# Routing the results of the first mixture layer by twos, and a ninth addend in the gate sums

## The chip, the core and the metric

The kernel runs on one core of one Trainium2 chip. The metric is the time of one execution on the device, in microseconds (us), as the median of several runs. The engines are named as in the profile: PE (TensorE, matrix products), PEld (its weight loads), DVE (VectorE), ACT (ScalarE), POOL (GpSimd) and SP (SyncE, which issues most of the transfers).

## The reference

```
x = attention(q, k, v)                      # a decaying state, 2 x 768 tokens, 512 wide: 1536 rows
# first layer: 8 experts, each token to one of them, if x @ w_skip > 0
probs = exp(logits - max) ; probs /= probs.sum() + 1e-9
x[mask_e] += gate * (relu(x[mask_e] @ w1[e]) @ w2[e])
# second layer: a new choice of expert from the first layer's result, at most `capacity` rows each
out[i] = gate2 * (relu(x_i @ w1b[e]) @ w2b[e])
```

So the second layer's choice (the logits of the 512 wide row, their maximum, the gate, and the place of the row in its expert's list) must be worked out for every row that leaves the first layer. This is the routing that the change is about. A router pass has 128 rows: one expert of the first layer.

## The kernel before

Attention fills the first 70 us. Then the first layer goes through its 8 experts, 128 gathered rows each, and the second layer through its 8 experts in blocks of 128 rows. All matrix products of the layers are in three passes over operands that are split into a rounded part and a rest (hi and lo, 512 columns a matmul); six of them use up one half of a weight chunk. A few weight chunks stay whole and are used in plain fp32 (L825). Weights come in chunks of 1 MB on SP's queue; ACT rounds each half (L248), DVE takes the rest (L251), and the raw buffer is then free for the next chunk. `pump` puts one such half into the order at each turn, and `step_side` calls it.

The code is written in the order in which each engine executes: every engine keeps the order of its own instructions. The loop over expert e of the first layer runs: `layer1(e)`, 24 matmuls into s; `layer2(e - 1)`, matmuls into o, with the transposes of the next expert's rows x after the first six (`turned`, L761); then the transposes of layer 1's result h (hT, eight, L761). `turned` and all routing products use one ring of three PSUM buffers, t.

`route_b(e)` routes the result of expert e. It is a generator in the list `side`: one step of it per turn, each between two groups of six matmuls. Its steps: DVE forms the result row (L846); PE transposes it (L860, four), ACT copies it (L862); PE forms the logits on 32 columns (L866), ACT copies them (L868); PE sums the four partial logits (L871), and `pick` finds maximum, choice m and gate on DVE and ACT; PE counts the place in the list (`ranked`, L327 and L328, which need m and the running count cumb); DVE turns the place into a one-hot matrix whereb (L889); PE adds row numbers to the table of slots (`to_slots`, L341). For expert e this runs beside `layer1(e + 2)`, since the result of expert e comes at the end of loop e + 1. The last two experts have a shorter course, since the second layer waits for them.

`gate` sums the eight exponentials (L320), adds 1e-9 (L322) and takes the reciprocal (L323).

Of the kernel before, what the change touches and what calls it, by code (L numbers as in the profile page):

```python
# [7 lines left out]
F32 = mybir.dt.float32  # L8
# [10 lines left out]
NTILE = NT // 128  # L19
# [22 lines left out]
def kernel(  # L42
# [88 lines left out]
    cum = const.tile([128, 2, 16], BF16, name="cum")  # L131
    cumb = const.tile([128, 8], BF16, name="cumb")
    cap = const.tile([1, 1], F32, name="cap")
    t9 = {n: const.tile([128, n, 9], F32, name=f"t9{n}") for n in (1, 2, 4)}


# [12 lines left out]
    def derived():  # L149

        for t in t9.values():
            nc.gpsimd.memset(t, 0.5)
        nc.gpsimd.memset(cum, 0.0)
# [138 lines left out]
    def pick(lg, nt, ng, rm, gate_out, ex=None, gate_first=False):  # L292

        n = nt * ng
        l4 = lg[:, :, 0:8 * ng].rearrange("p a (g j) -> p a g j", g=ng)
        mx = sm.tile([128, nt, ng, 1], F32, tag=f"mx{n}", name="mx")
        nc.vector.tensor_reduce(out=mx, in_=l4, axis=AX.X, op=ALU.max)
        d = sm.tile([128, n, 8], F32, tag=f"d{n}", name="d")
        d4 = d.rearrange("p (a g) j -> p a g j", a=nt)
        nc.vector.tensor_tensor(out=d4, in0=l4, in1=mx.to_broadcast([128, nt, ng, 8]), op=ALU.subtract)  # L300
        if rm is None:
            rm = taken(lg, nt)
        if ex is None:
            ex = sm.tile([128, n, 8], F32, tag=f"ex{n}", name="ex")
        nc.scalar.activation(out=ex, in_=d, func=ACTF.Exp)
        t = t9[n]
        nc.vector.scalar_tensor_tensor(out=t[:, :, 0:8], in0=d, scalar=0.0, in1=rm, op0=ALU.is_equal, op1=ALU.mult)
        if gate_first:
            gate(ex, nt, ng, gate_out)
        tm = sm.tile([128, n, 1], F32, tag=f"tm{n}", name="tm")  # L310
        nc.vector.tensor_reduce(out=tm, in_=t, axis=AX.X, op=ALU.max)
        m = sm.tile([128, n, 8], BF16, tag=f"m{n}", name="m", bufs=3)
        nc.vector.tensor_tensor(out=m, in0=t[:, :, 0:8], in1=tm.to_broadcast([128, n, 8]), op=ALU.is_equal)

        return m, lambda: gate(ex, nt, ng, gate_out)

    def gate(ex, nt, ng, gate_out):
        n = nt * ng
        se = sm.tile([128, nt, ng, 1], F32, tag=f"se{n}", name="se")
# [63 lines left out]
    def route_tokens(rows, rows_p):  # L383
# [94 lines left out]
        def last_chunk(xt, psum):  # L478
# [5 lines left out]
            ex = sm.tile([128, 2 * B, 8], F32, tag="exl", name="exl", bufs=1)  # L484
# [249 lines left out]
    w2_p = fast.enter_context(tc.tile_pool(name="w2", bufs=NW2))  # L734
    w_free += [(0, w2_p)] * NW2
    m_p = fast.enter_context(tc.tile_pool(name="m", bufs=2))
    row2 = [m_p.tile([128, RW], F32, name=f"row2{i}", bufs=1) for i in range(3)]
    for t in row2:
        nc.gpsimd.memset(t[:, DM:RW], 0.0)

    def psum(tag="t", bufs=3):
        return ps.tile([128, 512], F32, tag=tag, bufs=bufs, name=tag)
# [13 lines left out]
    def turned(src, g, tag, divided=True):  # L756

        pool = x_p if tag == "x" else m_p
        t = psum()
        for k in range(4):  # L760
            nc.tensor.transpose(t[:, 128 * k:128 * k + 128], src[:, 512 * g + 128 * k:512 * g + 128 * k + 128], ident)  # L761
        t = t.rearrange("p (k t) -> p k t", k=4)
        if divided:
            w = 128 if tag == "x" else 256
            hi = pool.tile([128, 4, w], F32R, tag=tag + "h", name=tag + "h")[:, :, 0:128]
            lo = pool.tile([128, 4, w], F32R, tag=tag + "l", name=tag + "l")[:, :, 0:128]
            split(t, hi, lo)
            return hi, lo
        as_is = pool.tile([128, 4, 128], F32, tag=tag + "w", name=tag + "w")
        nc.scalar.activation(out=as_is, in_=t, func=ACTF.Copy)  # L770
        return (as_is,)

# [66 lines left out]
            return True  # L839
        return uses.get(kind, 0) > 0  # L840

    def route_b(e, xs, acc, lead, rest):

        r2 = row2[e % 3]
        idc = xs[:, IDCOL:IDCOL + 1]
# [3 lines left out]
        nc.gpsimd.tensor_copy(out=r2[:, IDCOL:IDCOL + 1], in_=idc)  # L849
        if xs is not a0:  # L850
            xs_free.append(xs)
        there = sm.tile([128, 1], F32, tag="there", name="there")
        nc.gpsimd.tensor_scalar(out=there, in0=idc, scalar1=0.0, scalar2=None, op0=ALU.is_lt)
        rm = sm.tile([128, 1, 8], F32, tag="rmb", name="rmb")
        nc.gpsimd.tensor_scalar(out=rm[:, 0, :], in0=rev, scalar1=there, scalar2=None, op0=ALU.mult)
        yield
        yield from idle(lead)
        xr = psum()
        for k in range(KT):
            nc.tensor.transpose(xr[:, 128 * k:128 * k + 128], r2[:, 128 * k:128 * k + 128], ident)  # L860
        x2t = m_p.tile([128, KT, 128], F32, tag="x2t", name="x2t", bufs=1)
        nc.scalar.activation(out=x2t, in_=xr.rearrange("p (k t) -> p k t", k=KT), func=ACTF.Copy)  # L862
        yield
        lg = psum()
        for k in range(KT):
            nc.tensor.matmul(out=lg[32 * k:32 * k + 32, 0:128], lhsT=wgt[:, k, :], rhs=x2t[:, k, :], start=True, stop=True)  # L866
        lgs = sm.tile([128, 128], F32, tag="lgsb", name="lgsb")
        nc.scalar.activation(out=lgs, in_=lg[:, 0:128], func=ACTF.Copy)  # L868
        yield
        lt = psum()  # L870
        nc.tensor.matmul(out=lt[:, 0:8], lhsT=lgs, rhs=zsum[:, 8:16], start=True, stop=True)  # L871
        m, weigh = pick(lt[:, 0:8].unsqueeze(1), 1, 1, rm, r2[:, GCOL + 1:GCOL + 2].unsqueeze(1), None, e == E - 1)
        if e < E - 1:
            weigh()
        if e >= E - 2:
            write_rows(nc.scalar, r2.unsqueeze(1), 1)
        m = m[:, 0, :]
        rhs = sm.tile([128, 2, 8], BF16, tag="rhsb", name="rhsb")
        nc.gpsimd.tensor_scalar(out=rhs[:, 0, :], in0=m, scalar1=p1, scalar2=None, op0=ALU.mult)  # L879
        nc.gpsimd.tensor_scalar(out=rhs[:, 1, :], in0=m, scalar1=float(128 * (NTILE + e)), scalar2=None, op0=ALU.mult)  # L880
        yield from idle(1 + rest)
        rk = psum()
        ranked(rk, lc[:, 1, :], m, cumb)
        pr = sm.tile([128, 8], F32, tag="prb", name="prb")
        nc.vector.tensor_tensor(out=pr, in0=rk[:, 0:8], in1=m, op=ALU.mult)
        sl = sm.tile([128, 1], F32, tag="slb", name="slb")
        nc.vector.tensor_reduce(out=sl, in_=pr, axis=AX.X, op=ALU.add)
        where = sm.tile([128, 257], BF16, tag="whereb", name="whereb")
        nc.vector.tensor_scalar(out=where, in0=iota, scalar1=sl, scalar2=None, op0=ALU.is_equal)  # L889
        if e < E - 2:  # L890
            write_rows(nc.scalar, r2.unsqueeze(1), 1)
        nc.gpsimd.tensor_tensor(out=cumb, in0=cumb, in1=m, op=ALU.subtract)
        yield from idle(3 if e < E - 1 else 1)
        to_slots(where, rhs, 8, 8)
        yield

    def emit_out(xs, acc, shared=False):
# [30 lines left out]
        nc.vector.tensor_copy(out=flag, in_=over)  # L928
        return flag

    side = []
    pieces = [1]

    def step_side():
        for g in list(side):
# [27 lines left out]
        except StopIteration as stop:  # L963
            return stop.value

    def then_route(e, acc, lead, rest, between=lambda: None):
        g = route_b(e, xs1[e], acc, lead, rest)
        next(g)
        between()
        side.append(g)  # L970

    h0 = []
    first = layer1(x, "w1a", 0, h0)
# [10 lines left out]
    step_side()  # L984
    x = turned(xs1[1], 0, "x")
    acc = run(second)
    then_route(0, acc, 1, 1)
    for e in range(1, E):
        first = layer1(x, "w1a", e)
        if e == 1:  # L990
# [10 lines left out]
        if e > 1:  # L1001
            second = layer2(hT.pop(e - 1), "w2a", e - 1)
            next(second)
            step_side()
            x = turned(xs1[e + 1] if e + 1 < E else a0, 0, "x")
            if e == E - 1:

# [5 lines left out]
            then_route(e - 1, acc, *((2, 1) if e < E - 1 else (0, 0)), step_side)  # L1013
        hT[e] = run(turn)
    second = layer2(hT.pop(E - 1), "w2a", E - 1)
    for i in range(FT // 2):
# [1 line left out]
        pieces[0] = i < 2  # L1018
        step_side()
    acc = run(second)  # L1020
    last = route_b(E - 1, xs1[E - 1], acc, 0, 0)
    next(last)

    xs2 = {(0, 0): a0}

# [298 lines left out]
```

## Time and profile before

| | us |
|---|---|
| median of three runs (397.52 to 399.19) | 398.36 |
| the profiled execution | 395.72 |
| its span, first to last instruction | 393.9 |
| PE busy in it | 376.5 (96%) |
| DVE, ACT, POOL busy | 244.8, 210.5, 119.9 |

A row of the timeline has the start and the length of an instruction, engine, line and operation, result and operand, and the number of instructions merged. The ends of PE's matmuls are modelled, so what a group of PE instructions costs is read from start to start: from its first to the first of the next group.

### The profile page before, as it was taken

To read this page: it belongs to the slowest core of one execution; us is meant where nothing else is said; L and a number is where in the kernel's file an instruction comes from. 1 tells how busy PE (TensorE), PEld (TensorE's weight loads), DVE (VectorE), ACT (ScalarE), POOL (GpSimd) and SP (SyncE) were. 2 spreads that over 40 slices of the span, in tenths; PEclk is the share of its full clock that TensorE was granted. 3 is DMA by queue.
4 is the path that set the end of the run, shared out by engine and by line. 5 is a ranking of instruction groups with operands and counts; after the bars stand their busy time and mean duration, and the time that the engine had idled before them with its cause. 6 is when DMAs were issued, how large, how long until landed. Compare 5 with 4: busy or idle time off the path is not lost. (4 is left out here: it accounts for less than half of the span.)

```text
span 393.9 us, 6866 instructions
## 1 busy us (share of the span) xinstructions
PE 376.5 (96%) x2664; PEld 309.0 (78%) x2664; DVE 244.8 (62%) x437; ACT 210.5 (53%) x319; POOL 119.9 (30%) x184
## 2 busy tenths in 40 slices
PE   8999999899989999998999999999999999999992
PEld 4788887786667677676567998989989898898981
DVE  3657767498889869869535964654826476373200
ACT  1435655388778748747326753636636465462201
POOL 3678854262504402202143201304022040311102
PEclk9999999999999999999999999999999999999997
DMA  8999973899999998889844773965739377110101
GB/s 303 416 419 404 333 251 146 278 329 376 347 426 351 303 352 307 286 314 311 292 162 117 264 276 113 277 245 175 252 136 342 126 229 275 61 54 5 48 3 41
DMA packets 18175, 95.98 MB, mean 244 GB/s; under 512 B 2449, under 2 KB 2705, under 8 KB 8664
## 3 DMA queue, kind: packets, MB, share of 16 engines
q1 hardware_dynamic: 12196, 80.85, 56.5%
q0 software_dynamic: 3280, 9.76, 8.0%
q10 hardware_dynamic: 2660, 4.86, 3.3%
q8 instruction: 23, 0.38, 0.4%
q14 instruction: 16, 0.13, 0.1%
HBM read 87.03 MB, written 9.48 MB: 245 GB/s over the span
## 5 line engine op out<-in xcount | busy, mean ns | idle before, releaser
L251 DVE TENSOR_TENSOR lo<-big,hi 128x1024 fp32r<-128x1024 f32 (+1 forms) x126 | 147.5, 1185 | 60.9 <-ACT hi L248 60.0
L248 ACT ACTIVATE hi<-big 128x1024 fp32r<-128x1024 f32 (+1 forms) x126 | 124.6, 1013 | 3.8 <-DMA big<-in_w2a_dram 1.7
L784 PE MATMUL s<-xh,lo 128*128 128x256 f32 x224 | 63.4, 283 | 0.0
L783 PE MATMUL s<-xl,hi 128*128 128x256 f32 x224 | 63.4, 283 | 0.0
L782 PE MATMUL s<-xh,hi 128*128 128x256 f32 x224 | 63.4, 283 | 0.0
L905 POOL DMA_INDIRECT out_dram<-y,ixo x16 | 18.6, 1162 | 142.4 <-ACT y L900 139.4
L782 PE MATMUL o<-hi,hTh 128*128 128x512 f32 x112 | 44.9, 401 | 0.0
L783 PE MATMUL o<-lo,hTh 128*128 128x512 f32 x112 | 44.4, 396 | 0.0
L784 PE MATMUL o<-hi,hTl 128*128 128x512 f32 x112 | 44.4, 396 | 0.0
L782 PEld LDWEIGHTS s<-xh,hi 128*128 128x128 f32 x224 | 42.9, 191 | 0.3
L783 PEld LDWEIGHTS s<-xl,hi 128*128 128x128 f32 x224 | 42.9, 191 | 0.3
L784 PEld LDWEIGHTS s<-xh,lo 128*128 128x128 f32 x224 | 42.9, 192 | 0.0
L1084 ACT ACTIVATE hTh<-s 128x512 fp32r<-128x512 f32 x28 | 16.8, 598 | 41.0 <-PE s L784 41.0
L1085 DVE SCALAR_TENSOR_TENSOR hTl<-s,hTh 128x512 fp32r<-128x512 f32 x28 | 19.3, 691 | 30.5 <-ACT hTh L1084 30.3
L790 PE MATMUL s<-hi,xh 128*128 128x512 f32 x80 | 34.3, 429 | 1.6 <-DVE xl L377 0.9
L900 ACT ACTIVATE y<-o,rowc 128x512 f32<-128x512 f32 (+1 forms) x15 | 10.1, 674 | 47.6 <-issue 30.6
L790 PE MATMUL s<-lo,xh 128*128 128x512 f32 x80 | 31.5, 394 | 0.0
L879 POOL TENSOR_SCALAR rhsb<-m,cs 128x8 bf16<-128x8 bf16 x8 | 2.5, 306 | 81.1 <-DVE se L320 76.6
L790 PE MATMUL o<-hi,hTh 128*128 128x512 f32 x64 | 26.6, 415 | 0.0
L790 PE MATMUL o<-lo,hTh 128*128 128x512 f32 x64 | 25.3, 396 | 0.0
L784 PEld LDWEIGHTS o<-hi,hTl 128*128 128x128 f32 x112 | 21.1, 188 | 5.1
L790 PE MATMUL s<-hi,xl 128*128 128x512 f32 x80 | 25.1, 394 | 0.0
(162 smaller groups left out, 635.6 us busy)
## 6 DMA issues: line engine op xcount, KB each, us to landing
big<-in_w1a_dram SPq DMA_DIRECT2D x16, 1024.0 KB, 7.7
big<-in_w2a_dram SPq DMA_DIRECT2D x16, 1024.0 KB, 7.2
big<-in_w1b_dram SPq DMA_DIRECT2D x16, 1024.0 KB, 7.1
big<-in_w2b_dram SPq DMA_DIRECT2D x16, 1024.0 KB, 5.1
qk<-in_qkv_dram SPq DMA_DIRECT2D x5, 1024.0 KB, 10.2
big<-in_qkv_dram SPq DMA_DIRECT2D x5, 1024.0 KB, 12.0
table<-rowc ACTq DMA_DIRECT2D x5, 516.0 KB, 6.3
table<-row ACTq DMA_DIRECT2D x8, 258.0 KB, 7.2
```

Of the source, the lines that this page charges most:

```text
L248: nc.scalar.activation(out=hi[:, k], in_=r3[:, k], func=ACTF.Copy)
L251: nc.vector.tensor_tensor(out=lo[:, k], in0=r3[:, k], in1=hi[:, k].bitcast(F32), op=ALU.subtract)
L782: nc.tensor.matmul(out=acc, lhsT=a[0], rhs=w[0], start=first, stop=False)
L783: nc.tensor.matmul(out=acc, lhsT=a[0], rhs=w[1], start=False, stop=False)
L784: nc.tensor.matmul(out=acc, lhsT=a[1], rhs=w[0], start=False, stop=last)
L790: nc.tensor.matmul(out=acc, lhsT=a, rhs=w, start=first and i == 0, stop=last and i == len(todo) - 1)
L879: nc.gpsimd.tensor_scalar(out=rhs[:, 0, :], in0=m, scalar1=p1, scalar2=None, op0=ALU.mult)
L900: nc.scalar.activation(out=y[:, 0:n], in_=acc[:, 0:n], func=ACTF.Copy, scale=xs[:, GCOL + 1:GCOL + 2])
L905: new = nc.gpsimd.indirect_dma_start(out=out[:, :], out_offset=bass.IndirectOffsetOnAxis(ap=ix, axis=0), in_=y, in_offset=None, bounds_che ...
L1084: nc.scalar.activation(out=hi[:, g:g + 2, :], in_=acc, func=ACTF.Relu)
L1085: nc.vector.scalar_tensor_tensor(out=lo[:, g:g + 2, :], in0=acc, scalar=0.0, in1=hi[:, g:g + 2, :].bitcast(F32), op0=ALU.max, op1=ALU.subtract
```

## The change

Experts 0 and 1, and 2 and 3, are routed together, in a second list of generators, `sited`. It is stepped at two sites of each loop: just before x is transposed, and just before h is transposed. So a couple's course spreads over three loops. Experts 4 and 5 are routed together too, but in the old list and places; 6 and 7 go alone as before. The result row itself moves into a function of its own and stays where it was. The rows of two experts stand side by side in a tile (two tiles for two, in place of three for one), and each step works on both: eight transposes, two copies, logits 256 columns wide, two sums, one choice. The count for the second expert of a couple is the running count less the first one's choice, so `ranked` now needs a GpSimd subtraction that itself needs m (tile cu). In the gate sums the exponentials stand in a tile with a ninth column that holds 1e-9 from the start, and the addition (L322) goes.

```
     def gate(ex, nt, ng, gate_out):
-        sf = sm.tile([128, nt, ng], F32, tag=f"sf{n}", name="sf")
-        nc.vector.tensor_scalar(out=sf, in0=se.rearrange("p a g o -> p a (g o)"), scalar1=1e-9, scalar2=None, op0=ALU.add)
-        nc.vector.reciprocal(out=gate_out, in_=sf)
+        nc.vector.reciprocal(out=gate_out, in_=se.rearrange("p a g o -> p a (g o)"))
...
-    row2 = [m_p.tile([128, RW], F32, name=f"row2{i}", bufs=1) for i in range(3)]
+    row2 = [m_p.tile([128, 2, RW], F32, name=f"row2{i}", bufs=1) for i in range(2)]
...
+    def route_b(es, lead, rest):
+        n, e = len(es), es[0]
+        r2 = row2[e // 2 % 2][:, e % 2:e % 2 + n, :]
...
         yield from idle(lead)
+        x2t = m_p.tile([128, 2, KT, 128], F32, tag="x2t", name="x2t", bufs=1)
+        for i in range(n):
+            xr = psum()
+            for k in range(KT):
+                nc.tensor.transpose(xr[:, 128 * k:128 * k + 128], r2[:, i, 128 * k:128 * k + 128], ident)
+            nc.scalar.activation(out=x2t[:, i], in_=xr.rearrange("p (k t) -> p k t", k=KT), func=ACTF.Copy)
         yield
...
+            nc.tensor.matmul(out=lg[32 * k:32 * k + 32, 0:128 * n], lhsT=wgt[:, k, :], rhs=x2t[:, 0:n, k, :], start=True, stop=True)
...
+        nc.gpsimd.tensor_copy(out=cu[:, 0, :], in_=cumb)
+        for i in range(1, n):
+            nc.gpsimd.tensor_tensor(out=cu[:, i, :], in0=cu[:, i - 1, :], in1=m[:, i - 1, :], op=ALU.subtract)
...
+    def then_route(e, acc, between=lambda: None):
+        result(e, xs1[e], acc)
+        between()
+        if e % 2 and e < E - 3:
+            sited.append(route_b([e - 1, e], 1, 0))
+        elif e == E - 3:
+            side.append(route_b([e - 1, e], 2, 1))
+        elif e == E - 2:
+            side.append(route_b([e], 0, 0))
...
             step_side()
+            site()
             x = turned(xs1[e + 1] if e + 1 < E else a0, 0, "x")
...
+        site()
         hT[e] = run(turn)
```

PE before, in `layer1` of expert 3, beside which expert 1 is routed (row is its result, x2t the transposed copy, wgt the router's weights; the lines are those of the kernel before):

```order
L860 MATMUL t<-cs,row_1164 128x128 x4
L790 MATMUL s<-hi,xh 128x512
L790 MATMUL s<-lo,xh 128x512
L790 MATMUL s<-hi,xh 128x512
L790 MATMUL s<-lo,xh 128x512
L790 MATMUL s<-hi,xl 128x512 x2
L866 MATMUL t<-x2t,wgt 32x128 x4
L790 MATMUL s<-hi,xh 128x512
```

PE now, in `layer2` of expert 2 in the same loop, at the first site that the couple of experts 0 and 1 uses (the lines are those of the changed kernel; L868 are the couple's transposes, L763 those of x, L792 the matmuls of L790):

```order
L792 MATMUL o<-hi,hTl 128x512 x2
L868 MATMUL t<-cs,row_1151 128x128 x8
L763 MATMUL t<-cs,rowc_108 128x128 x4
L792 MATMUL o<-hi,hTh 128x512
L792 MATMUL o<-lo,hTh 128x512
L792 MATMUL o<-hi,hTh 128x512
```

The transposes of the result have left the matmuls into s, and stand eight together ahead of those of x; the 24 matmuls into s follow each other without a break.

PE now, at the end of loop 6 and the start of loop 7: the count of experts 2 and 3, h's transposes, and the transposes of experts 4 and 5, in the old place:

```order
L330 MATMUL t<-cu,ones 128x16
L763 MATMUL t<-cs,h 128x128 x8
L792 MATMUL s<-hi,xh 128x512
L792 MATMUL s<-lo,xh 128x512
L792 MATMUL s<-hi,xh 128x512
L792 MATMUL s<-lo,xh 128x512
L792 MATMUL s<-hi,xl 128x512 x2
L868 MATMUL t<-cs,row_1151 128x128 x8
```

Eight transposes stand where four did, after the same six matmuls, and they take two buffers of the ring t: counted from h's first half they are its third and fourth users, so the second four reuse the buffer of h's first half.

DVE now at the same place (L847 is the result of expert 5, L899 to L905 the slots of experts 2 and 3, L379 the lower part of h's two halves, L301 the start of the choice for experts 4 and 5):

```order
L255 TENSOR_TENSOR lo<-big_86,hi 128x1024
L847 SCALAR_TENSOR_TENSOR row_1151<-o,rowc_108 128x512
L899 TENSOR_TENSOR prb<-t,m 128x16
L901 TENSOR_REDUCE slb<-prb 128x2
L905 TENSOR_SCALAR whereb<-iota,slb 128x257 x2
L379 TENSOR_TENSOR hTl<-t,hTh 128x4x128 x2
L255 TENSOR_TENSOR lo<-big_86,hi 128x1024
L301 TENSOR_REDUCE mx<-t 128x2
```

The slots of the couple before now stand between the result of expert 5 and the two subtractions for h; before, hTl came right behind the result.

## Rows read from the trace of the kernel before

**Rows 1.** Windows, the first layer and the second (busy us, instructions; clock, DMA).

```profile
86.00:200.00 114.00, 108.93 (x587) 78.19 (x586) 92.54 (x165) 77.68 (x114) 28.05 (x50) 1.00 0.93 334
200.00:378.00 178.00, 176.89 (x1127) 159.22 (x1126) 96.36 (x114) 88.24 (x118) 36.86 (x44) 1.00 0.50 169
```

**Rows 2.** Timeline of PE, 140 to 154: the routing of expert 3.

```profile
140.41 0.40 PE L790 MATMUL s<-lo,xh 128*128 128x512 f32 x1
140.65 0.62 PE L790 MATMUL s<-hi,xl 128*128 128x512 f32 x2
141.23 0.66 PE L860 MATMUL t<-cs,row 128*128 128x128 f32 x4
141.64 0.47 PE L790 MATMUL s<-hi,xh 128*128 128x512 f32 x1
...
142.65 0.63 PE L790 MATMUL s<-hi,xl 128*128 128x512 f32 x2
143.20 0.43 PE L866 MATMUL t<-x2t,wgt 128*32 128x128 f32 x8
143.56 0.50 PE L790 MATMUL s<-hi,xh 128*128 128x512 f32 x1
143.90 0.40 PE L790 MATMUL s<-lo,xh 128*128 128x512 f32 x1
...
145.08 0.28 PE L871 MATMUL t<-zsum,lgsb 128*128 128x8 f32 x2
145.22 0.48 PE L790 MATMUL s<-hi,xh 128*128 128x512 f32 x1
...
148.09 0.18 PE L327 MATMUL t<-m,lc 128*128 128x8 bf16 x1
...
148.16 0.63 PE L761 MATMUL t<-cs,rowc 128*128 128x128 f32 x4
...
152.85 0.26 PE L341 MATMUL tab<-rhsb,whereb 128*128 128x8 bf16 x4
152.96 1.07 PE L761 MATMUL t<-cs,h 128*128 128x128 f32 x8
```

**Rows 3.** Waits, 86 to 184: who waited for whom, us, times, longest.

```profile
PEld t L860 <- DVE row L846: 4.7, 6, 1.5
...
PE t L860 <- DVE row L846: 2.3, 4, 1.1
...
PE t L327 <- DVE m L313: 0.6, 1, 0.6
```

**Rows 4.** Timeline of PE, 57 to 59.5: two tiles' logits in attention.

```profile
57.55 0.64 PE L389 MATMUL s<-xt,wgt 128*32 128x256 f32 x8
58.12 0.72 PE L622 MATMUL s<-qk 64*128 64x128 f32 x8
58.76 0.62 PE L399 MATMUL s<-zsum,lgs 128*128 128x18 f32 x4
59.23 0.47 PE L663 MATMUL m<-qk,sbd 128*128 128x128 f32 x2
```

**Rows 5.** Timeline of all engines, 105 to 109.2: expert 3's x.

```profile
105.50 1.06 ACT L248 ACTIVATE hi<-big 128x1024 fp32r<-128x1024 f32 x1 [1.73 <-DMA big<-in_w2a_dram]
...
107.73 0.68 DVE L377 TENSOR_TENSOR xl<-t,xh 128x512 fp32r<-128x512 f32 x1
...
109.00 0.47 PE L790 MATMUL s<-hi,xh 128*128 128x512 f32 x1
```

**Rows 6.** Timeline of DVE, 150 to 156: slots, and the next result.

```profile
150.80 0.36 DVE L889 TENSOR_SCALAR whereb<-iota,slb 128x257 bf16<-128x257 f32 x1
...
155.08 0.75 DVE L846 SCALAR_TENSOR_TENSOR row<-o,rowc 128x512 f32<-128x512 f32 x1
```

**Rows 7.** Timeline of POOL, 147 to 164: what follows a choice.

```profile
147.39 0.31 POOL L879 TENSOR_SCALAR rhsb<-m,cs 128x8 bf16<-128x8 bf16 x1 [9.64 <-DVE se L320]
...
163.03 0.75 POOL L892 TENSOR_TENSOR cumb<-cumb,m 128x8 bf16<-128x8 bf16 x1 [0.36 <-PE t L328]
```

More of the change, by code (lines that the diff above doesn't have):

```diff
@@ L133 @@
     cap = const.tile([1, 1], F32, name="cap")
+    ex9 = {n: const.tile([128, n, 9], F32, name=f"ex9{n}") for n in (1, 2, 4)}
     t9 = {n: const.tile([128, n, 9], F32, name=f"t9{n}") for n in (1, 2, 4)}
@@ L152, in derived @@
             nc.gpsimd.memset(t, 0.5)
+        for t in ex9.values():
+            nc.gpsimd.memset(t, 1e-9)
         nc.gpsimd.memset(cum, 0.0)
@@ L840, in done_with, with result @@
         return uses.get(kind, 0) > 0
-    def route_b(e, xs, acc, lead, rest):
-        r2 = row2[e % 3]
-        idc = xs[:, IDCOL:IDCOL + 1]
+    def result(e, xs, acc):
+        r2 = row2[e // 2 % 2][:, e % 2, :]
         nc.vector.scalar_tensor_tensor(
@@ L865, in route_b @@
         for k in range(KT):
[L866 to L868 removed]
+            nc.tensor.matmul(out=lg[32 * k:32 * k + 32, 0:128 * n], lhsT=wgt[:, k, :], rhs=x2t[:, 0:n, k, :], start=True, stop=True)
+        lgs = sm.tile([128, 256], F32, tag="lgs", name="lgs")
+        nc.scalar.activation(out=lgs[:, 0:128 * n], in_=lg[:, 0:128 * n], func=ACTF.Copy)
         yield
         lt = psum()
[L871 to L872 removed]
+        for i in range(n):
+            nc.tensor.matmul(out=lt[:, 8 * i:8 * i + 8], lhsT=lgs[:, 128 * i:128 * i + 128], rhs=zsum[:, 8:16], start=True, stop=True)
+        m, weigh = pick(
+            lt[:, 0:8 * n].rearrange("p (a j) -> p a j", a=n), n, 1, rm, r2[:, :, GCOL + 1:GCOL + 2], None, e == E - 1
+        )
         if e < E - 1:
@@ L875, in route_b @@
         if e >= E - 2:
[L876 to L880, printed above, removed]
+            write_rows(nc.scalar, r2, n)
+        rhs = sm.tile([128, n, 2, 8], BF16, tag=f"rhsb{n}", name="rhsb")
@@ new lines, in route_b @@
+        cu = sm.tile([128, n, 8], BF16, tag=f"cu{n}", name="cu")
+        nc.gpsimd.tensor_copy(out=cu[:, 0, :], in_=cumb)
+        for i in range(1, n):
+            nc.gpsimd.tensor_tensor(out=cu[:, i, :], in0=cu[:, i - 1, :], in1=m[:, i - 1, :], op=ALU.subtract)
+        nc.gpsimd.tensor_scalar(out=rhs[:, :, 0, :], in0=m, scalar1=p1, scalar2=None, op0=ALU.mult)
+        for i in range(n):
+            nc.gpsimd.tensor_scalar(out=rhs[:, i, 1, :], in0=m[:, i, :], scalar1=float(128 * (NTILE + es[i])), scalar2=None, op0=ALU.mult)
@@ L887, in route_b @@
+        sl = sm.tile([128, n], F32, tag=f"slb{n}", name="slb")
         nc.vector.tensor_reduce(out=sl, in_=pr, axis=AX.X, op=ALU.add)
-        where = sm.tile([128, 257], BF16, tag="whereb", name="whereb")
-        nc.vector.tensor_scalar(out=where, in0=iota, scalar1=sl, scalar2=None, op0=ALU.is_equal)
+        where = []
+        for i in range(n):
+            where.append(sm.tile([128, 257], BF16, tag="whereb", name="whereb"))
+            nc.vector.tensor_scalar(out=where[i], in0=iota, scalar1=sl[:, i:i + 1], scalar2=None, op0=ALU.is_equal)
@@ L890, in route_b @@
         if e < E - 2:
[L891 to L894, printed above, removed]
+            write_rows(nc.scalar, r2, n)
+        nc.gpsimd.tensor_tensor(out=cumb, in0=cu[:, n - 1, :], in1=m[:, n - 1, :], op=ALU.subtract)
+        yield from idle(1 if e < E - 4 or e == E - 1 else 3)
+        for i in range(n):
+            to_slots(where[i], rhs[:, i], 8, 8)
@@ L929, in overflow, with site @@
         return flag
-    side = []
+    side, sited = [], []
     pieces = [1]
+    def site():
+        for g in list(sited):
+            try:
+                next(g)
+            except StopIteration:
+                sited.remove(g)
     def step_side():
@@ L986 @@
     acc = run(second)
[L987 removed]
+    then_route(0, acc)
     for e in range(1, E):
@@ L1020 @@
     acc = run(second)
-    last = route_b(E - 1, xs1[E - 1], acc, 0, 0)
-    next(last)
+    result(E - 1, xs1[E - 1], acc)
+    last = route_b([E - 1], 0, 0)
     xs2 = {(0, 0): a0}
```

47 lines of the change are left out of this document (18 added, 29 removed).

## The prediction

> **What bounds the kernel.** I read three views in this order. The windows first: in the first layer PE is busy for 108.93 of 114 us at full clock, in the second for 176.89 of 178 [rows 1]. So PE sets the end, and a microsecond that PE saves in the first layer is saved at the end, as long as nothing that feeds PE becomes late: behind it stand only products that PE runs without a gap. But DVE is busy for 92.54 of those 114 us, ACT for 77.68, and the transfer engines for 0.93 of the time [rows 1]. The reader should see that the spare time of the feeders is small in this stage. Second, the timeline of PE from start to start, to price one routing [rows 2]. Third, the waits: in the first layer PE waits for little but the result row and the choice [rows 3]. What it waits for there is on the routing's own chain, which is why moving the routing can pay more than its instructions.
>
> **What one routing costs PE** [rows 2]. A regular matmul takes 0.24 (140.41 to 140.65). The transposes: 141.23 to 141.64 is 0.41, or 0.10 each; the first matmul behind a foreign group comes late, by 0.34 less 0.24 = 0.10 behind the logits (143.56 to 143.90), and I take 0.08 behind the other groups, an estimate from that; 0.49. The logits: 0.36 themselves (143.20 to 143.56), 0.07 ahead of them (142.65 plus two matmuls is 143.13) and 0.10 behind; 0.53. The sums: 0.14 and 0.08; 0.22. The count stands beside x's transposes, the slots beside h's: 0.07 and 0.11, each with about 0.03 more; 0.10 and 0.14. Together 1.48, and 8.9 for the six experts 0 to 5. Of expert 0 I take off 0.2: its sums stand ahead of h's transposes, which wait for ACT's copy of h anyway. That leaves 8.7.
>
> **The waits that go.** Transposes that wait for the result row cost PE between 2.3 (PE idle) and 4.7 (weight loads idle), and the count of expert 0 waits 0.6 for its choice [rows 3]. In the routing of rows 2 the transposes start at 141.23, 0.11 behind the two matmuls from 140.65, so that one hardly waits; the waits are uneven, with 1.1 the longest on PE. The ends of PE's matmuls are modelled, so I take 4.0 for all, between 2.9 and 5.3. At the sites the couple's result rows are at least one layer's 24 matmuls old, and nothing waits for them. Removed in all: 12.7.
>
> **What comes instead.** At a site the eight transposes stand ahead of x's: 8 x 0.10 = 0.8, without a late matmul of their own. The logits with 256 columns take 0.57 in attention (57.55 to 58.12) [rows 4], and beside h's transposes I add 0.15 for the change over: 0.72 (0.57 to 0.77). Two sums: 0.28 and 0.03 (attention's two, with 18 columns each, take 0.47 [rows 4], which is the upper end). The count is as dear for 16 columns as for 8, bounded by the 0.07 and twice that: 0.10. Eight slots: 0.22 and 0.03. Sum 2.2 for a couple, 4.4 for the two. Experts 4 and 5 keep the old places: 0.9 + 0.74 + 0.36 + 0.10 + 0.30 = 2.4. Added in all: 6.8. Net of instructions and old waits: 5.9 faster.
>
> ACT copies as much as before, its two copies in a row; DVE does seven short instructions of `pick` and `gate` for two experts where it did sixteen, so it has about 2 us less work a couple. The ninth column costs a few GpSimd fills at the start, while the first loads are under way, and the addition that goes was on DVE, not on PE's path. Were that cover gone, the fills would cost under 0.5 and the addition's end would be worth 0.2 at the last expert, where the choice stands behind the gate. The doubled table writes move the same bytes on ACT's queue, later, and the couple's rows of expert 0 and 2 a whole loop later; they are wanted only by the second layer. The single buffer of the plain hT tile is refilled two loops later. I take 0 for all of these, within 0.3 either way.
>
> **What may be late next.** (a) Expert 3's x. Its lower part is formed from 107.73 to 108.41, and PE takes it up at 109.00, 0.6 later [rows 5]. ACT had waited 1.73 for a weight chunk until 105.50, ahead of x's copy in its queue [rows 5]. With expert 0's routing gone PE arrives 2.5 earlier (1.3 of instructions and 1.2 of waits). If the landing keeps its time, PE waits 1.9; if it moves up with DVE, whose work frees the buffer for that chunk, it waits for nothing. DVE is freed of expert 0's choice and slots ahead of it, nearly as much time, so I take 0.4. (b) The transposes of expert 5. They need the PSUM buffer of h's first half, and DVE reads that last behind the result row and now behind the couple's slots too. In the loop of rows 2 the result row started at 155.08 [rows 6], 2.2 behind the last o at 152.85 [rows 2]. Then the row (0.7), the slots (0.36 for each one-hot matrix [rows 6], with the two small instructions about 1.0) and the subtraction (0.7) end 4.6 behind that o. PE wants the buffer after eight transposes, six matmuls and four transposes, 0.8 + 1.5 + 0.4 = 2.7 behind it. So the wait is 1.9 if DVE is as late as there, and none if DVE is free when o ends (then 2.5). DVE has less to do in loop 6 than before, since no choice stands beside its slots; I take 0.4. (c) The count now stands behind a GpSimd subtraction that waits for the choice; behind it on PE stand h's transposes or the slots, and all that follows. For experts 4 and 5 the count comes 12 matmuls behind the sums, 2.87 (145.22 to 148.09) [rows 2]. GpSimd's first instruction behind the choice started at 147.39, 2.17 behind that, and took 0.31; such a subtraction took up to 0.75 [rows 7]. So the count is free at 2.5 to 2.9: wait 0 to 0.1, taken as 0. At the sites there is more time, with x's transposes and ten matmuls between.
>
> The 0.75 was measured while DVE ran a subtraction of 1024 columns, the 0.31 while it did not [rows 7]. The Trainium skill, "SBUF — State Buffer", section "SBUF: two separate sides", says that DVE instructions with two SBUF inputs and GpSimd instructions share a port pair as an exclusive lock, held for a whole instruction. The longer row agrees in kind. By that rule, if DVE's next weight subtraction got the pair first, the count would wait for some 1.2 us more, a wait of about 1.0 there and a sum of 4.1 for 5.1; since the subtraction follows the choice at once and DVE still has two small instructions to do, I leave it at 0.
>
> **Sum.** 5.9 less 0.8 of new waits: 5.1 faster. The profiled execution, 395.72 (its span 393.9 and 1.8 around it), would become 390.6. The median of the runs is 398.36, 2.6 above it, and I take the same difference from it: 393.3.
>
> **Rivals.** First, the new waits take most of it: (a) 1.9, (b) 1.9 and (c) 1.0 at their upper ends, 4.8 in place of 0.8, leave 1.1 faster, 397.3; typically two of them, about 2.5 faster, 395.9. For it: the 0.6 us of lead in rows 5, and DVE busy for four fifths. Against it: each of them happens once, and DVE's load falls. Second, the weights become the bound. The transfer engines work for 0.93 of 114 us [rows 1], that is 106 us, and the stage would need 109 after the forecast; if they can't get above 0.93, PE just waits for weights and the time stays at 398. Against it: PE never waits for a weight half in this profile, and ACT waits for a landing only rarely, so the lead is in the buffers. Third, slower: ACT's order. At the sites two copies of results, and in front of them two rounded weight halves that may wait for a landing, now stand ahead of the copy of x, on which the next layer 1 depends. If in each of the loops 2 to 7 ACT stood for 1.73 as at 105.50 [rows 5] with PE waiting for all of it, that is 10.4 against 5.9 saved: 4.5 slower, 402.9. It decides from a loss of about 1.0 a loop on. For it: the loops get shorter by about a tenth while landings do not. Against it: x has some five microseconds from its transposes to its use, and before the change a wait of 1.73 cost PE nothing.
>
> **Chances.** Forecast 0.66, waits 0.20, weights 0.09, slower 0.05. A difference below 0.5%, or 2 us, can't be told from none. The forecast is nearly all in faster, of the waits two thirds: faster 0.79, same 0.16, slower 0.05. The best case is 5.3 of old waits and no new ones: 1.3 and 0.8 more, 391.2. The worst within the first rival is 397.3. With a little cut off at both ends the range is 391.4 to 397.0.
>
> **What would show it.** In the profile after: the first layer's s groups of 24 without a break in loops 2 to 6; transposes of the couples 0 to 3 with no wait for the result row; logits at 0.57 for two; the first s of loop 3 right behind h's transposes (a late one there is (a)); the second four transposes of experts 4 and 5 right behind the first (b); the count right behind the matmuls (c). PE's busy share in the first layer should rise, and the stage shrink by about 5. It would be wrong if PE shows new gaps in front of matmuls into s or o, or if ACT's waits for landings grow beyond the 1.73.

## The result, and the profile after

The changed kernel takes **393.36 us** (median of 13 runs, 389.4 to 396.76) where the kernel before takes 397.74 (13 runs, 395.5 to 399.46): ratio 0.9884, 95% interval 0.9855 to 0.9912, 4.4 us or 1.2% faster. The forecast was 393.3. The medians in this document are over all runs; the ratios leave out the disturbed ones.

Windows of the changed kernel, columns as in [rows 1]:

```profile
86.00:200.00 114.00, 109.55 (x569) 81.55 (x568) 90.07 (x136) 78.46 (x110) 26.35 (x52) 0.99 0.91 335
200.00:378.00 178.00, 177.34 (x1128) 159.83 (x1127) 94.83 (x109) 87.57 (x116) 36.82 (x44) 1.00 0.50 169
```

PE is busier (109.55 for 108.93) although it does fewer things: the second layer begins earlier and fills the window, and some matmuls run at the lower clock (below). DVE has 29 instructions and 2.5 us less. The transfer engines still work for 0.91 of the time.

The couple of experts 0 and 1 at its sites, in the timeline of PE (start, duration, engine, line, result and operands, form, count); it answers to [rows 2]:

```profile
114.00 1.04 PE L868 MATMUL t<-cs,row 128*128 128x128 f32 x8
114.87 0.60 PE L763 MATMUL t<-cs,rowc 128*128 128x128 f32 x4
...
119.05 0.63 PE L792 MATMUL o<-hi,hTl 128*128 128x512 f32 x2
119.60 0.64 PE L873 MATMUL t<-x2t,wgt 128*32 128x256 f32 x8
120.17 1.09 PE L763 MATMUL t<-cs,h 128*128 128x128 f32 x8
...
127.99 0.51 PE L879 MATMUL t<-zsum,lgs 128*128 128x8 f32 x4
128.35 0.63 PE L763 MATMUL t<-cs,rowc 128*128 128x128 f32 x4
```

Read start to start: the eight transposes take 0.87, with no idle time ahead; the logits 0.57, and they come 0.09 late behind the last two matmuls; the four sum matmuls 0.36. The groups of 24 matmuls into s of experts 3 to 6 run unbroken, 5.54 to 5.57 us each, as forecast.

Where the stage gained and lost is best seen from landmarks: the first s of an expert's layer 1 and the first o of its layer 2, read from the timeline of PE. Differences of these starts, us; "again" and "third" are two more profiles of the changed kernel, "both" is the best version below (experiment 7), and block 2 is the second block of rows of the second layer's first expert:

```
from          to                      before   after   again   third   both
s expert 0    s expert 1               12.86   12.83   12.85   12.84   12.84
s expert 1    s expert 3               22.86   20.23   20.23   20.23   20.23
s expert 3    s expert 4               15.30   14.00   14.74   14.58   13.99
s expert 4    s expert 5               15.33   13.51   13.83   13.51   13.52
s expert 5    s expert 6               14.16   14.22   14.26   14.21   14.22
s expert 6    s expert 7               15.23   13.52   13.51   13.52   13.51
s expert 7    o expert 6                6.94   11.54    8.59    8.63    7.10
o expert 6    second layer, block 2    33.04   33.12   33.11   33.08   33.79
sum                                   135.72  132.97  131.12  130.60  129.20
```

Up to expert 7's s the change gains 6.3 to 7.4 us; behind it, where experts 4 and 5 are routed in the old place, it gives 1.7 to 4.7 back. The first profile is the worst of the three there:

```profile
162.27 0.48 PE L792 MATMUL s<-hi,xh 128*128 128x512 f32 x1
...
163.28 0.61 PE L792 MATMUL s<-hi,xl 128*128 128x512 f32 x2
165.13 0.66 PE L868 MATMUL t<-cs,row 128*128 128x128 f32 x4 [1.24 <-DVE prb L899]
166.47 1.12 PE L868 MATMUL t<-cs,row 128*128 128x128 f32 x4 [0.69 <-ACT x2t L869]
167.24 0.78 PE L792 MATMUL s<-hi,xh 128*128 128x512 f32 x1
167.81 0.63 PE L792 MATMUL s<-lo,xh 128*128 128x512 f32 x1
168.24 0.63 PE L792 MATMUL s<-hi,xh 128*128 128x512 f32 x1
```

DVE in the same stretch, cut off at 166.2 (it answers to [rows 6]), and ACT:

```profile
163.10 1.22 DVE L255 TENSOR_TENSOR lo<-big,hi 128x1024 fp32r<-128x1024 f32 x1 [1.41 <-ACT hi L252]
164.25 0.74 DVE L847 SCALAR_TENSOR_TENSOR row<-o,rowc 128x512 f32<-128x512 f32 x1
164.91 0.16 DVE L899 TENSOR_TENSOR prb<-t,m 128x16 f32<-128x16 f32 x1
...
165.84 0.68 DVE L379 TENSOR_TENSOR hTl<-t,hTh 128x512 fp32r<-128x512 f32 x1
```
```profile
162.01 1.06 ACT L252 ACTIVATE hi<-big 128x1024 fp32r<-128x1024 f32 x1 [1.58 <-DMA big<-in_w1b_dram]
...
165.82 0.60 ACT L869 ACTIVATE x2t<-t 128x512 f32<-128x512 f32 x1 [1.78 <-PE t L868]
```

Two waits stand here. The first four transposes start 0.06 behind the end of `prb` (165.07), DVE's last reading of the count's buffer, which stands behind the result row in DVE's queue. That queue had waited 1.41 for ACT's rounding of a weight half, and ACT 1.58 for the landing (the arrival from memory) of that chunk. The second four start at 166.47, 0.05 behind the end of ACT's copy of the first four (166.42), and before the first `hTl` has ended (166.52). So they don't wait for the buffer of h's first half, as the section on the change and the prediction have it: they go into the buffer of the first four (experiment 9 has a clearer case). Behind both the matmuls step by 0.43 instead of 0.23: the clock fell. Windows over the stretch show it (PE's idle time, then the granted clock, the last column but two):

```profile
163.50:167.00 3.50, 1.58 (x9) 0.95 (x8) 3.43 (x8) 1.14 (x3) 0.00 (x0) 0.90 0.89 320
167.00:170.00 3.00, 3.00 (x13) 2.10 (x15) 0.13 (x1) 0.60 (x1) 0.00 (x0) 0.54 1.00 399
```

0.54 is nearly the lower level, 1.2 GHz of 2.4. The six matmuls there take 2.7 us, in the other profiles 1.55; the four transposes ahead of them take 0.77, in the other profiles 0.41.

### The profile page after: what moved, and what is told of

Its sections match the earlier page's. It is cut to its first block, busy times and chain, and to the rows that moved or that the text cites. A ratio compares the mean times of both kernels' runs of the same rounds, so it can differ in the third digit from the quotient of the medians.

```text
span 391.5 us, 6763 instructions
## 1 busy us (share of the span) xinstructions
PE 375.3 (96%) x2634; PEld 311.5 (80%) x2634; DVE 239.2 (61%) x396; ACT 209.9 (54%) x313; POOL 117.2 (30%) x185
## 5 line engine op out<-in xcount | busy, mean ns | idle before, releaser
L792 PE MATMUL s<-hi,xh 128*128 128x512 f32 x80 | 33.5, 418 | 1.6 <-DVE xl L379 0.9
L792 PE MATMUL s<-lo,xh 128*128 128x512 f32 x80 | 31.8, 397 | 0.0
L792 PE MATMUL o<-hi,hTh 128*128 128x512 f32 x64 | 26.5, 415 | 0.0
L792 PE MATMUL o<-lo,hTh 128*128 128x512 f32 x64 | 25.3, 396 | 0.0
L792 PE MATMUL s<-hi,xl 128*128 128x512 f32 x80 | 25.2, 396 | 0.0
L784 PEld LDWEIGHTS o<-hi,hTh 128*128 128x128 f32 x112 | 21.0, 188 | 4.8
```

The lines of the kernel that those rows point to most:

```text
L784: nc.tensor.matmul(out=acc, lhsT=a[0], rhs=w[0], start=first, stop=False)
L792: nc.tensor.matmul(out=acc, lhsT=a, rhs=w, start=first and i == 0, stop=last and i == len(todo) - 1)
```

## The experiments

**1. The changed kernel again** (no edit; `after_again`).

> The changed kernel once more, for a second profile of the same program. In the first profile loop 7 (from the first s of expert 7 to the first o of expert 6) takes 11.5 us, of which some 2.2 are waits of PE ahead of the transposes of experts 4 and 5, and some 1.4 matmuls at the lower clock behind them. Theory A (these waits belong to the place: the result row of expert 5 and the PSUM buffer of h's first half both hang on VectorE's queue): they are there again, each within 0.5 us of the first time. Theory B (a weight landing of this one execution): loop 7 takes about 8 us, with 0.5 us of waits or less and a full clock. Time either way about 393.4.

Measured: 392.59 us, ratio 0.9865 (0.9833 to 0.9896). Half of each theory. The wait between the two sets of transposes is there again, the other one and the lower clock are not:

```profile
165.69 0.60 PE L868 MATMUL t<-cs,row 128*128 128x128 f32 x4
166.97 0.66 PE L868 MATMUL t<-cs,row 128*128 128x128 f32 x4 [0.69 <-ACT x2t L869]
```

From the fourth to the fifth transpose it is 0.96 (0.11 without a wait), exactly as in the first profile: 0.85 lost. It is the time from the fourth transpose to ACT's copy and that copy itself, which took 0.60 from 166.32 in this profile and ended 0.05 ahead of the fifth. A loss that the first profile did not have stands in loop 4, on ACT and on PE:

```profile
118.92 1.06 ACT L252 ACTIVATE hi<-big 128x1024 fp32r<-128x1024 f32 x1 [3.23 <-DMA big<-in_w1a_dram]
119.88 1.06 ACT L869 ACTIVATE x2t<-t 128x512 f32<-128x512 f32 x2
```
```profile
121.00 0.64 PE L873 MATMUL t<-x2t,wgt 128*32 128x256 f32 x8 [0.48 <-ACT x2t L869]
```

ACT stands for a landing (the first half of expert 5's first chunk) with the copies of the result behind it in its queue, and PE's logits wait for these. In the first profile ACT stood there 2.64 and PE lost nothing.

**2. Experts 4 and 5 two steps later** (`late45`).

```diff
-            side.append(route_b([e - 1, e], 2, 1))
+            side.append(route_b([e - 1, e], 4, 0))
```

> The routing of experts 4 and 5 starts two steps (12 matmuls, 2.8 us) later, and its count stands one step nearer to its sums. Theory A (waits of the place): the result row and both PSUM buffers are ready by then, loop 7's waits of 2.2 us and its 1.4 us at the lower clock go, loop 7 drops from 11.5 to 8 or less, and the kernel is 2.2 to 3.6 us faster than the changed kernel, 390 to 391. Theory B (a landing of one execution): no difference beyond 0.5 us. Theory C (weights set the stage's end): loop 7 gets shorter, PE waits as much for weight halves in the loops behind it, and the time stays at 393.4.

Measured: 391.01 us, ratio 0.9853 (0.9821 to 0.9885); 1.6 us less than the changed kernel on the same chip by the medians, but the intervals of the two ratios overlap, so the trace has to tell it. From expert 7's s to expert 6's o it is 7.09 instead of 8.59, of which 0.7 comes back behind it (33.80 for 33.1; sums and count stand there now). Here DVE frees the buffer of the second four, long before they come. Theory A in kind, below its lower end in size. In this profile PE lost 1.3 ahead of the logits of experts 0 and 1, again behind a landing (3.05 on ACT).

**3. One at a time at the sites** (`sites_single`).

```diff
-        if e % 2 and e < E - 3:
-            sited.append(route_b([e - 1, e], 1, 0))
+        if e < E - 4:
+            sited.append(route_b([e], 1, 0))
```

> Experts 0 to 3 are routed one at a time, each at the sites (beside the transposes of x and h); 4 and 5 as in the changed kernel. So it has the sites without the couples. From the loops of the changed kernel a couple costs PE 1.52 for transposes and logits, 0.49 for sums and count, 0.21 for slots: 2.2, or 1.1 for one expert; one alone should cost 0.44 + 0.54 + 0.17 + 0.10 + 0.11 = 1.36 in those places. Theory A (the gain comes from the sites, where nothing is waited for): 4 x 0.25 = 1 us slower than the changed kernel, about 394.4, and still 3 us and more faster than before. Theory B (the gain comes from the couples, half as many instructions and change overs): 3 us or more slower than the changed kernel, 396.5 or above.

Measured: 399.65 us, ratio 1.0051 (1.0021 to 1.0080): slower than the kernel before. By the time alone that is theory B; the trace says otherwise. ACT and DVE, and what PE does meanwhile:

```profile
121.15 1.06 ACT L252 ACTIVATE hi<-big 128x1024 fp32r<-128x1024 f32 x1 [2.96 <-DMA big<-in_w1a_dram]
...
123.89 0.58 ACT L869 ACTIVATE x2t<-t 128x512 f32<-128x512 f32 x1
```
```profile
122.24 1.23 DVE L255 TENSOR_TENSOR lo<-big,hi 128x1024 fp32r<-128x1024 f32 x1 [2.79 <-ACT hi L252]
123.39 0.16 DVE L301 TENSOR_REDUCE mx<-t 128x1 f32<-128x8 f32 x1
...
124.25 0.17 DVE L317 TENSOR_TENSOR m<-t,tm 128x8 bf16<-128x8 f32 x1
```
```profile
121.47 0.63 PE L792 MATMUL o<-hi,hTl 128*128 128x512 f32 x2
124.48 0.19 PE L329 MATMUL t<-m,lc 128*128 128x8 bf16 x1 [2.38 <-DVE m L317]
...
128.01 1.11 PE L763 MATMUL t<-cs,h 128*128 128x128 f32 x4 [1.16 <-ACT lgs L875]
```

It is the same landing. One expert at a time puts expert 0's choice into this loop; the choice stands on DVE behind the subtraction for that late half, the count waits for it, then come the copies and the lower clock (0.55 granted from 124 to 128.5, 0.69 to 133). From expert 3's s to expert 4's it takes 19.05 where the changed kernel takes 14.0 to 14.7.

**4. Couples in the old places** (`old_twos`).

```diff
-            sited.append(route_b([e - 1, e], 1, 0))
+            side.append(route_b([e - 1, e], 2, 1))
```

> The couples 0, 1 and 2, 3 are routed in the places that experts 4 and 5 have (transposes 6 matmuls into the next s), not at the sites. So it has the couples without the sites. Theory A (the place makes the waits): each of the two couples pays what 4 and 5 pay, 2.2 us of waits and 0.2 of change overs, 4.8 us slower than the changed kernel, about 398, with up to 2.8 more where the clock falls behind the waits: no gain over before, or a loss. Theory B (the couples make the gain): within 1 us of the changed kernel, 393.4 to 394.4.

Measured: 395.81 us, ratio 0.9942 (0.9907 to 0.9976), twelve runs from 392.12 to 398.55. Between the theories: the first couple waits long, the second not at all (eight transposes in 0.79), the third 1.1.

```profile
108.23 0.60 PE L868 MATMUL t<-cs,row 128*128 128x128 f32 x4
112.27 1.12 PE L868 MATMUL t<-cs,row 128*128 128x128 f32 x4 [3.44 <-ACT x2t L869]
```

**5. The late chunk taken up later, one at a time** (`sites_single_land`). The split of one half is issued four steps later; nothing is left out, and its bytes move as before.

```diff
-... and raw_t[i][1] + LANDING <= count["turn"]
+... and raw_t[i][1] + LANDING + 4 * (order[i][0] == ("w1a", 5, 0)) <= count["turn"]
```

> Experts 0 to 3 one at a time at the sites, as in the run that came out at 399.65, but the first half of expert 5's first weight chunk is taken up by ScalarE four steps later in its program, behind the copies of the result and of x instead of ahead of them. Theory A (that run lost its time to this one landing: ScalarE stood 2.96 us for it, VectorE's choice for expert 0 stood behind the second half of the same pair, and PE came back at the lower clock): 394 to 395.5, PE's wait for the choice of 2.4 us gone, the clock full in that loop. Theory B (one expert at a time costs that much more at the sites): 398 to 400, as without the edit.

Measured: 394.10 us, ratio 0.9927 (0.9901 to 0.9954). Theory A: the order of one rounding on ACT was worth some 5 us (5.5 by the medians, 4.9 by the ratios; the two runs were on different chips), and with it the sites without couples are 0.7% faster than before. The count now stands right behind the matmuls (from the timeline of PE):

```profile
120.35 0.63 PE L792 MATMUL o<-hi,hTl 128*128 128x512 f32 x2
120.82 0.18 PE L329 MATMUL t<-m,lc 128*128 128x8 bf16 x1
```

**6. The same delay, couples in the old places** (`old_twos_land`).

> The couples in the places between two groups of 6 matmuls into s, as in the run that came out at 395.81, with the same four steps of delay for the first half of expert 5's first chunk. That run's times fell into two groups, about 392.2 and about 396. Theory A (the upper group is one landing, which reaches PE through the copy of the result): all runs come near the lower group, 392 to 393, and the wait of 3.4 us between the two sets of four transposes in loop 4 is gone. Theory B (that wait is the PSUM buffer behind VectorE's queue, which has nothing to do with the landing): 395 to 396.5 as before the edit.

Measured: 396.06 us, ratio 0.9953 (0.9923 to 0.9983), with the wait between the two sets of transposes still there. Theory A fell for this landing. The time is theory B's, but its cause is not: the wait ends with ACT's copy, not with DVE. PE and ACT, 108 to 113:

```profile
108.46 0.60 PE L868 MATMUL t<-cs,row 128*128 128x128 f32 x4
112.27 0.76 PE L868 MATMUL t<-cs,row 128*128 128x128 f32 x4 [3.22 <-ACT x2t L869]
```
```profile
109.64 0.58 ACT L378 ACTIVATE hTh<-t 128x512 fp32r<-128x512 f32 x1
110.19 1.06 ACT L252 ACTIVATE hi<-big 128x1024 fp32r<-128x1024 f32 x1
111.15 0.58 ACT L378 ACTIVATE hTh<-t 128x512 fp32r<-128x512 f32 x1
111.63 0.59 ACT L869 ACTIVATE x2t<-t 128x512 f32<-128x512 f32 x1
```

The second four follow the end of ACT's copy by 0.05 in both runs. The copy came 2.8 us after its transposes, because h's two copies and a weight half stood ahead of it on ACT; in experiment 4 that half had waited 1.87 for another landing, here it had not, and the copy began at 111.62 and 111.63 all the same. I had delayed the wrong half, and ACT's arrears in that loop have more than one cause.

**7. Both edits, 2 and 5, on the changed kernel** (`late45_land`).

> The version with experts 4 and 5 two steps later (391.01), with the same delay for the first half of expert 5's first chunk. In its profile PE waits 1.32 us ahead of the logits of experts 0 and 1, for the copy of their transposes behind a landing of 3.05 us on ScalarE. Theory A (landing): this wait goes, 0.5 to 1.5 us faster, 389.5 to 390.5. Theory B (the landing only moves the wait on, to the weight halves that PE needs next): no faster than 391, with PE waiting in front of matmuls into s of expert 5.

Measured: **389.84 us**, ratio 0.9834 (0.9796 to 0.9872). Theory A by the trace; by the time alone it can't be told from experiment 2, since the intervals of the ratios overlap. From expert 3's s to expert 4's it takes 13.99, and the waits of PE in the first layer, 86 to 180, are two:

```profile
PE t L868 <- DVE row L847: 0.8, 1, 0.8
PE t L763 <- ACT h L815: 0.2, 1, 0.2
```

**8. Only the ninth addend, on the kernel before** (`sum9`).

```diff
+            ex = ex9[n]
+        nc.scalar.activation(out=ex[:, :, 0:8], in_=d, func=ACTF.Exp)
...
-        nc.vector.tensor_scalar(out=sf, in0=se..., scalar1=1e-9, scalar2=None, op0=ALU.add)
```

> The kernel before with nothing but the ninth column: the exponentials are written into a tile whose ninth column holds the small term, and the addition between the sum and the reciprocal goes. Theory A (the addition is VectorE's, off PE's path): within 0.5 us of the kernel before, 396.7. Theory B (VectorE, busy four fifths of the first layer, passes on 0.16 us for each of the eight choices there and those of attention): 1 to 2 us faster, 395 to 395.7.

Measured: 397.91 us beside 397.51, ratio 1.0028 (0.9996 to 1.0059). Theory A: nothing.

**9. Expert 5's transposes in another buffer** (`xr_o`). Theory A is the prediction's: h's first half behind VectorE.

```diff
-            xr = psum()
+            xr = psum("o", 2) if e == E - 4 and i else psum()
```

> The changed kernel, with the four transposes of expert 5 in a buffer of layer 2's accumulators (the one of expert 4, long read) instead of the ring of three. Theory A (in loop 7 the second four transposes wait for the ring's buffer, which holds h's first half until VectorE has read it): the step of 0.96 us from the fourth to the fifth transpose shrinks to 0.11, the stretch from the first s of expert 7 to the first o of expert 6 goes from 8.59 to 7.7, and the time falls by 0.85 us, to about 392; the trace tells it, the time hardly can. Theory B (they wait for the result row of expert 5, or for ScalarE's copy of the first four, which the profile names): the step stays near 0.96.

Measured: 391.81 us, ratio 0.9882 (0.9845 to 0.9920). The second four follow 0.5 behind the first, without a wait (0.11 from fourth to fifth): it was the buffer.

```profile
168.89 0.66 PE L868 MATMUL t<-cs,row 128*128 128x128 f32 x4 [0.87 <-DVE prb L899]
169.39 0.60 PE L868 MATMUL o<-cs,row 128*128 128x128 f32 x4
```

Which buffer, the ends tell: in all three profiles of the changed kernel the second four start 0.05 behind the end of ACT's copy of the first four, and 0.03 to 0.05 ahead of the end of the first `hTl`. That margin is small, but experiment 3 has the same eight transposes with one one-hot matrix less ahead of `hTl` on DVE. DVE there, and PE:

```profile
174.40 1.28 DVE L379 TENSOR_TENSOR hTl<-t,hTh 128x512 fp32r<-128x512 f32 x2
```
```profile
175.30 0.66 PE L868 MATMUL t<-cs,row 128*128 128x128 f32 x4 [0.69 <-ACT x2t L869]
```

One such subtraction takes 0.68, so DVE has read h's first half at 175.08, and PE waits until 175.30 all the same, 0.05 behind ACT's copy (174.65 to 175.25): the step stays at 0.96. In experiment 4, where the second four of experts 4 and 5 wait for their row, they start 0.23 behind the beginning of the first `hTl`, long before its end. So of theory A only the first half holds, and B's second candidate, ACT's copy, was the right one.

The other wait, ahead of the first four, is here in this profile, 1.0, behind `prb` again: the stretch is 8.84, not 7.7. It has the first profile's cause. On ACT stands:

```profile
165.78 1.06 ACT L252 ACTIVATE hi<-big 128x1024 fp32r<-128x1024 f32 x1 [1.22 <-PE t L330]
```

The profile puts this wait down to PE's count, but it is the same rounding, and in the trace the semaphore of its chunk's landing rises 0.10 ahead of it, as in the first profile (0.11). The chunk is issued 7.6 us ahead of expert 7's s in all four profiles; it landed 0.4 and 0.7 ahead of that s in the first profile and here, 2.7 and 2.8 ahead in "again" and "third", where the wait is missing. Why the transfer takes 7 us in some executions and 5 in others stays open.

**10. Experts 4 and 5 one at a time** (`singles45`). Here the sums of expert 4 stand ahead of the count of 2 and 3, so that the ranks of 4 and 5 leave those two out and the second layer gets other rows; so the time is no comparison, and only the first layer is read.

```diff
-        elif e == E - 3:
-            side.append(route_b([e - 1, e], 2, 1))
+        elif E - 5 < e < E - 2:
+            side.append(route_b([e], 2, 1))
```

> Couples 0, 1 and 2, 3 at the sites as in the changed kernel; experts 4 and 5 one at a time, as in the kernel before. Theory A (the couple of 4 and 5 saves some 0.6 us of instructions and loses 0.85 us to its buffer): within 1 us of the changed kernel, 392.4 to 394.4; the s group of expert 6 goes from 5.57 to 7 to 7.5, that of expert 7 from 8.59 to 6.95. Theory B (the couple in this place costs what the first profile of the changed kernel shows, 4.6 us more than one expert alone): 1.5 to 3 us faster than the changed kernel, 390 to 392.

Measured: 394.15 us, ratio 0.9935 (0.9911 to 0.9959). From expert 6's s to expert 6's o it is 23.00 (6.86, 8.19, 7.95), for 22.10 and 22.15 in profiles "again" and "third" and 25.06 in the first. So the couple is 0.9 cheaper even with its buffer wait in those two profiles, and 2.1 dearer in the first: theory A, though its 6.95 for the s of expert 7 came out at 7.95. In that stretch the first four transposes wait 1.1 (start to start) behind `prb` here too, without a landing: in this program the choice of experts 2 and 3, and with it ACT's rounding behind it, comes 1.2 later before that s than in "again".

**11, 12. The changed kernel and both edits, side by side** (`after_third`, `both_third`).

> The changed kernel a third time, beside the version with both edits on the same chip. By the theory that its loss sits in two places, PE's wait ahead of the logits of experts 0 and 1 (0, 0.55 and 1.3 to 1.6 us in the profiles so far) and the 0.85 us or more ahead of the transposes of expert 5, both are in its profile again. Time 392 to 393.5.

> The version with experts 4 and 5 two steps later and the first half of expert 5's first chunk taken up later, again. If both edits take away waits of the program: neither of the two waits in the profile, 1.5 to 3 us faster than the changed kernel beside it, 389.5 to 391. If the earlier 389.84 owed something to that chip: less than 1 us faster.

Measured: 392.65 us, ratio 0.9905 (0.9875 to 0.9935), and 391.23, ratio 0.9844 (0.9820 to 0.9868): 1.4 us apart by the medians, less than I expected (0.6%, or 2.4 us, by the ratios, whose intervals just don't overlap). The changed kernel has both waits again (0.3 at the logits, 0.7 at the transposes), the other neither; its profile has instead 0.4 for a choice and 0.2 for GpSimd's subtraction ahead of the count of experts 0 and 1, and from expert 4's s to expert 5's it takes 14.50 there, 1.0 more than in the first profile of the same version:

```profile
PE t L329 <- DVE m L317: 0.4, 1, 0.4
...
PE t L330 <- POOL cu L891: 0.2, 1, 0.2
```

## Why the prediction was right, and where it was not

**The time and the sum.** 393.3 forecast, 393.36 measured: that they agree so closely is luck. The sum took 5.1 off a median of three runs, 398.36; over 13 runs the kernel before takes 397.74 and the change saves 4.4, so that an error of 0.6 and one of 0.7 cancel. The step "5.1 faster" for the profiled execution was 2.4 in the first profile's span, 3.5 and 5.4 in the other two (393.9 to 391.5, 390.4, 388.5). The first layer alone, which the sum is about, shrank by 2.75, 4.60 and 5.12; attention ahead of it, which the change hardly touches, began it at 73.3 before and at 74.0, 74.8 and 73.4 after. The new waits, taken at 0.8, were some 3.7 (with the clock), 1.9 and 1.4 in the three profiles, so that the first profile lies near the first rival's case (2.5 faster) and not near the forecast's.

**One routing, and the couple.** The couple's terms came out as worked out: transposes 0.87 (0.8), logits 0.66 with the late start (0.72), sums 0.36 (0.31), slots 0.22 (0.25). Removing expert 0's routing with its waits gave 2.63 in the stretch from expert 1's s to expert 3's, for 1.3 of instructions and 1.2 of waits.

**The waits that go.** Up to expert 7's s the forecast is 6.6 to 7.0 faster: 12.7 removed, less 1.5 of expert 5, 4.2 for the couples without the last slots, and 0.4 for (a) or none. Measured 7.4, 6.3 and 6.8; with the landing out of the way ("both") 7.4. So the 4.0 us for old waits fits, though the stretches don't tell it apart from the instruction terms.

**(a) Expert 3's x.** Taken at 0.4 in a range of 0 to 1.9; it was 0, the first s follows h's transposes at once. It answers to [rows 5]:

```profile
106.78 0.49 PE L763 MATMUL t<-cs,h 128*128 128x128 f32 x3
107.03 0.47 PE L792 MATMUL s<-hi,xh 128*128 128x512 f32 x1
```

**(b) The buffer of expert 5's transposes** is the step that failed. "They need the PSUM buffer of h's first half, and DVE reads that last": the runs showed that they take the buffer of the first four, which ACT reads, so that the wait is 0.85 in all three profiles, and not between 0 and 1.9 by DVE's state (taken: 0.4). What I left out stands beside it: ahead of the first four I expected no wait, since [rows 2] showed hardly one, but there was one of 1.4 us (start to start) in the first profile, of 1.0 in those of experiments 9 and 10 and none in "again" and "third". There PE does stand behind DVE's queue, for the buffer of the count. In the first profile and in experiment 9 that queue had stood for ACT's rounding, and ACT for the landing of one and the same chunk; in experiment 10, another program, the queue was late without a landing. I also counted no clock: its fall cost 1.5 us in the first profile, 1.1 in the six matmuls and 0.4 in the transposes ahead of them.

**(c) The count** was free, as taken, in all but one place: in "again" that of experts 0 and 1 came 0.3 late (13.83 for 13.51 in the table). GpSimd's subtraction took 0.20 for both couples in the first profile's loops 6 and 7, and it was over before DVE's next subtraction of 1024 columns began. Behind the count, where nobody waits, the next subtraction on GpSimd took 1.01 us, at 176.54, while DVE's from 176.26 ran for 1.24. The Trainium skill, "SBUF — State Buffer", section "SBUF: two separate sides", has an exclusive lock between DVE's instructions with two SBUF inputs and GpSimd's, the rule that I had left at 0. This row agrees with it.

```profile
174.39 0.20 POOL L891 TENSOR_TENSOR cu<-cu,m 128x8 bf16<-128x8 bf16 x1 [11.19 <-DVE se L324]
...
176.54 1.01 POOL L908 TENSOR_TENSOR cumb<-cu,m 128x8 bf16<-128x8 bf16 x1
```

**The rivals.** The third (ACT's order and a landing) I gave 0.05 and priced over six loops. It happens in loop 4, and in the first profile in loop 7 too (the 1.58 above): in each of the three profiles of the changed kernel ACT stands in loop 4 for 2.6 to 3.5 us up to 117 to 119, and PE loses 0 to 0.55 at the logits (1.3 and 1.6 in the profiles of experiments 2 and 9). So a sign that I had named for being wrong, landings beyond 1.73, came in all three, and the time held all the same. My reason against it, that ACT waits for a landing only rarely, held for the old pace alone: the stage became faster and its weights did not ([rows 5] has 1.73 as its longest). Experiments 3 and 5 show how near it was: with one expert at a time the same landing costs some 5 us and makes the kernel slower than before. PE never waited for a weight half itself, so the second rival did not come.

**What gained.** Couples alone (experiment 4) 0.6%, sites alone 0.7% with experiment 5's delay, both 1.2%, the ninth addend nothing. Experts 4 and 5 are a couple in the old place in all three, so these shares are of experts 0 to 3 and need not add up.

## What to carry to other kernels

Price a routing or any such chain start to start on the busy engine, and add the waits of that chain from the trace: the sum held within a microsecond in the median, though not in each execution (2.75 to 5.12 in the first layer). Then ask for each moved step what stands in front of it in the in-order queues of its feeders, a weight that may be late above all: moving one rounding behind two copies was worth some 5 us in one version. When a stage gets shorter, landings that the old pace hid come to light (1.73 at most on ACT before, 2.6 to 3.5 after), and they cost most where a choice hangs on them.

## What the runs showed of the hardware that I had not expected

After the longer pauses of PE the granted clock fell, and such a pause cost more than itself. With PE busy for 1.58 of 3.5 us the next 3 us were at 0.54; after an idle 0.69 with PE busy on both sides it stayed at 1.00. Behind the 3.44 us of experiment 4 six matmuls took 2.75 instead of 1.55. The first layer's beginning also moves from execution to execution, 73.3 to 76.2 us, without any edit to what stands ahead; in some profiles (once more the changed kernel, experiment 1) the clock from 10 to 20 us was 0.75, in others 1.00, and one that began at 76.2 had a full clock there, so that the clock is not all of it.
